# Attention with a gated feed-forward on one core: some softmax tiles turned by VectorE and DRAM in place of TensorE

## The chip, the core and the metric

The kernel runs on one of the eight cores of a Trainium2 chip. A core has TensorE (matrix products into PSUM), VectorE, ScalarE and GpSimd (element-wise work), SyncE, whose queue issues most transfers, and 16 DMA engines that carry them between DRAM and SBUF, or within either. The engines run beside each other and wait for one another by semaphores. The metric is the device time of one execution in microseconds (us).

## The reference

Eight batches, eight heads, 576 tokens, 64 columns a head. For each batch and head the scores are q k^T / 8. Scores more than tau = 0.02 below the maximum of their row are masked; a softmax follows and a product with v. The heads' results, side by side 512 wide, go through a feed-forward block with a convolution over the tokens as its gate. In short:

```
scores = scale * np.matmul(q, k.transpose(0, 1, 3, 2))
thresh = np.max(scores, axis=-1, keepdims=True) - tau
scores = np.where(scores >= thresh, scores, -1000000000.0)
scores = scores - np.max(scores, axis=-1, keepdims=True)
attn = np.exp(scores)
attn = attn / (np.sum(attn, axis=-1, keepdims=True) + 1e-09)
x = np.matmul(attn, v)                                # then heads side by side: 512 columns
h = np.maximum(x @ w_in, 0.0)                         # 512 -> 1024
conv_out[t] = sum over k of conv_w[k] * h[t + k - 1]  # 3 taps
gate = 1.0 / (1.0 + np.exp(-conv_out))
out = h * gate @ w_out                                # 1024 -> 512
```

## The kernel before

**Tiles and stages.** Heads are taken in four pairs of heads per batch, tokens in five tiles (four of 128 rows, one of 64). A batch is cut into two chunks, tiles (0, 1) and tiles (2, 3, 4). A *unit* is one tile of one pair of heads: 20 a batch, 160 in all. `unit` (from L516) makes, for each of the two heads, the scores in PSUM (L537 in batch 0 and for the 64-row tiles, L544 elsewhere, where q is held as a rounded part and a rest that are multiplied one after the other), then VectorE's maximum (L552), a limit from it (L558, or L556 on ScalarE), ScalarE's exponential (L561), VectorE's mask with the sum (L564), a few one-column instructions (L581, L585, L588) and the normalisation (L595 on ScalarE, L597 on VectorE or GpSimd). The result stands in a buffer `em` of 128 rows by 2 x 576 columns, of which there are four.

**The turn.** The product with v needs the softmax with its columns on the partitions. `transposes` (from L608) lets TensorE turn `em` in blocks of 128 x 128: two groups of four blocks per full tile, and a last group (L652) with the ninth block of each full tile and what the 64-row tile leaves over. Each group is turned into a PSUM buffer (L626), which ScalarE copies to `eT` (L621). `eT` has nine blocks by up to 320 columns for one pair of heads and one chunk; there are two such buffers.

**After the turn.** `attend` (from L664) multiplies v with `eT` (L676, L685), after the first two chunks for two pairs of heads together, and splits the result into a rounded part and a rest, `x` (L692, L695). `mm1` (L701) is the first product of the feed-forward with the convolution and the gate, whose first tap goes to an engine by the list `TAP`; `mm2` (L777) the second product, an output copy by ScalarE (L793) and the store (L794).

**Loads and copies.** All loads after the first go through SyncE's queue. `prep_k` and `prep_q` (L483, L497) load k and q for two heads, split them into a rounded part and a rest, and copy halves of them to the other 64 partitions through the queue (L477): three copies of 64 KB for q's rounded part and three for its rest. The weights, which arrive as 64-bit numbers, are taken apart by `split` (L342).

**The order.** Nothing is left to run time: a planner in the kernel (`Plan`, L87 to L242) simulates the engines while the program is built and emits each engine's instructions in the order of that simulation. Each operation is given an engine, an assumed duration, what it reads and writes, and a rank. The rank is the number of the unit it belongs to, less a lead from the table `AHEAD`, in units: 6.25 for scores, 3.5 for the turn and for the attention. An engine takes the ready operation of the lowest rank. Some operations may be taken by another engine, when the backlog of ready work on their own exceeds `BACKLOG`:

```
if e == home or load[home] + max(free[home] - t, 0.0) > BACKLOG[home]:
```

The normalisation's own engine comes from the list `NORM`, which names GpSimd alone:

```
turns = NORM[u >= NEAR]
home = turns[(u * 2 + h) % len(turns)]
```

Because the order is fixed, an operation that is late holds up all that follows on its engine's queue, SyncE's included.

Of the kernel before, what the change touches and what calls it, by code (L numbers as in the profile page):

```python
# [41 lines left out]
EARLY = 1  # L42
# [6 lines left out]

JOINT = 2  # L50

KEEP = {'rows': 2.304, 'cols': 1.613, 'turn': 3.226, 'full': 2.304}
# [30 lines left out]
class Plan:  # L83
# [32 lines left out]
    def run(self):  # L116
# [35 lines left out]
        while events:  # L152
# [25 lines left out]
            for e in ready:  # L178
# [4 lines left out]
                while ready[e]:  # L183
# [6 lines left out]
                    if e == home or load[home] + max(free[home] - t, 0.0) > BACKLOG[home]:  # L190
# [55 lines left out]
def tile_tau_attention_gated_ffn(  # L246
# [80 lines left out]
    def sp(n):  # L327
        return 2.6 * n

# [12 lines left out]
    def split(src, n, name, high, low, hr, lr, queue="sp"):  # L342
# [4 lines left out]
        value = plan.buf(wk, "q2", 2, [P, 2, 2 * P], U32, f"{name}_f")  # L347
# [8 lines left out]
        def v(dtype=F32):  # L356
            return value[:].rearrange("p a b -> p (a b)")[:, :n].bitcast(dtype)

        lo, hi, a = (stage, 0), (stage, 1), (value, 0)
        w = AHEAD["w"]  # L360

        def load():
            (nc.sync if queue == "sp" else nc.scalar).dma_start(flat().bitcast(I64), src)
# [16 lines left out]
        if queue == "sp":  # L380
            op("sp", sp(2 * n), load, w=[hi, lo], ahead=w + AHEAD["load"])
        else:
            op("act", 450, load, w=[hi, lo], ahead=90, late=sp(2 * n) + LATENCY["sp"])
# [37 lines left out]
    def load_weight(i):  # L421
        if i < W1N:
            src, dst, c, f = w_in, w1, i % NCB, i // NCB
        else:
# [4 lines left out]
            src[c * P:(c + 1) * P, f], WN, f"stage_{i}", h, l, *((x, (c, f.start)) for x in dst), "act" if i < 3 else "sp"  # L429
# [14 lines left out]
    def prep_rows(i, b, p, o, w, tag):  # L444
# [3 lines left out]
        a = AHEAD["prep"]  # L448

        if i:  # L450
            op("sp", sp(S + D), lambda: nc.sync.dma_start(k[:], kp[b, p]), w=[(k, 0), (k, 1)], ahead=a + 2)
            op("sp", sp(2 * w), lambda: nc.sync.dma_start(q[:], qd[b, p, :, :, o:o + w]), w=[(q, 0), (q, 1)], ahead=a + 2)
        else:
            for j, on in enumerate((slice(0, CH), slice(CH, S + D))):
                op(
                    "act", 450, lambda on=on: nc.scalar.dma_start(k[:, on], kp[b, p, :, on]), w=[(k, j)], ahead=210 - 10 * j,
                    late=1500 + sp(CH) * (1 + j)
                )
                op(
                    "sp", sp(w) + 400, lambda j=j: nc.sync.dma_start(q[:, j], qd[b, p, :, j, o:o + w]), w=[(q, j)], ahead=210 - 10 * j  # L460
                )
# [7 lines left out]
    def halves(dst, src, of, ahead):  # L469

        x, view, parts = src
        for part, head in of:
            j, half = part
            n = view.shape[-1]
            op(
                "sp", max(sp(n) / 2, 360),
# [6 lines left out]
    def prep_k(b, p, ks):  # L483

        a = AHEAD["prep"]
        xk = plan.buf(wk, "xk", 2, [P, S + D], F32, f"xk_{b}_{p}")
        op("sp", sp(S), lambda: nc.sync.dma_start(xk[:, :S], kt[b, p]), w=[(xk, 0), (xk, 1)], ahead=a + 2)
# [9 lines left out]
    def prep_q(i, b, p, q1, q2):  # L497

        w, o = QW, chunks[pairs[i][0]].new[0]
        xq = plan.buf(wk, "xq", 2, [P, w], F32, f"xq_{i}")  # L500
        a = AHEAD["prep"]
        op("sp", sp(w), lambda: nc.sync.dma_start(xq[:], qt[b, p, :, o:o + w]), w=[(xq, 0)], ahead=a + 2)
# [5 lines left out]
        for q in (q1, q2):  # L508
            halves(q, (q, Later(lambda q=q: q[:, 0], w), ((0, 0), (0, 1))), [((1, 1), 1), ((1, 0), 1), ((0, 1), 0)], a)
# [318 lines left out]
    def prep(i, j):  # L828
# [4 lines left out]
        if plain(b):  # L833
            if not j:
                whole[i] = (*prep_rows(i, b, p, o, w, "q1"), None)
# [119 lines left out]
```

## Time and profile before

| | |
|---|---|
| Median of 3 runs | 927.24 us (926.33 to 927.37) |
| Profiled execution | 925.54 us, span of its instructions 923.8 us |
| Granted TensorE clock, mean | 0.996 |
| Busy share of the span | TensorE 97%, VectorE 80%, ScalarE 76%, GpSimd 63% |
| Transfers | 104.02 MB in 77926 packets, mean 113 GB/s |
| HBM | 58.88 MB read, 9.44 MB written |

In the profile a line such as L626 is the line of the kernel that issued the instruction. PE is TensorE's matmuls and PEld its loads of the stationary operand, DVE is VectorE, ACT ScalarE, POOL GpSimd, SP SyncE; an engine's name with a q behind it is its queue of transfers or waits. `eT<-ps_t` reads as: writes the tile eT from the tile ps_t. Busy times within a group of instructions can overlap with those of other groups on the same engine, because instructions are pipelined.

### The profile page before, as it was taken

How to read it: one execution, taken by the hardware profiler on the slowest of the kernel's cores; microseconds unless marked ns; L12 is line 12 of the kernel's file. 1: busy time of each engine (PE TensorE's matmuls, PEld its weight loads, DVE VectorE, ACT ScalarE, POOL GpSimd, SP SyncE). 2: the span in 40 equal slices, each digit the busy share in tenths (PEclk: the TensorE clock that was granted, in tenths of full speed). 3: DMA queues.
4: the chain of work that ended last, by engine and by line, in shares of the span. 5: the costliest groups of instructions: out<-in, count | busy, mean ns of one | idle time of the engine just before them, and what ended most of it. 6: DMA issues, size and time to landing. Idle time of an engine off the chain costs nothing.

```text
span 923.8 us, 19667 instructions
## 1 busy us (share of the span) xinstructions
PE 896.7 (97%) x6308; PEld 731.8 (79%) x6308; DVE 741.1 (80%) x1853; ACT 701.2 (76%) x1590; POOL 582.1 (63%) x1028
## 2 busy tenths in 40 slices
PE   5989899999999999999999999999999999999998
PEld 2446588878889788879888787887888888887897
DVE  5988999979868798878967789886977879896643
ACT  5888898878678787869768687786958788785653
POOL 3665887767747586666746677675865757664422
PEclk9999999999999999999999999999999999999999
DMA  6643363355341652345423453416523265221000
GB/s 211 200 151 128 97 166 101 111 146 167 87 122 40 176 150 83 84 115 140 122 91 81 133 148 103 120 59 166 161 85 95 55 175 140 83 79 60 13 24 34
DMA packets 77926, 104.02 MB, mean 113 GB/s; under 512 B 18560, under 2 KB 49536, under 8 KB 77824
## 3 DMA queue, kind: packets, MB, share of 16 engines
q1 hardware_dynamic: 76960, 100.86, 38.6%
q10 hardware_dynamic: 864, 1.90, 0.6%
q8 instruction: 51, 0.84, 0.4%
q14 instruction: 51, 0.42, 0.1%
HBM read 58.88 MB, written 9.44 MB: 74 GB/s over the span
## 4 chain that ended last, share of the span: by engine, by line
PE 79%; ACT 9%; DVE 6%; issue 2%; DMA 2%; POOL 1%; SPq 0%; ACTq 0%; POOLq 0%; DVEq 0%
PE po L786 21%; PE ph L713 16%; PE ps_t L626 13%; PE pa L685 12%; PE ps_s L544 11%; PE ps_s L537 4%; ACT eT L621 2%; PE pa L676 2%; DVE em L564 2%; ACT em L561 2%; DVE few L552 1%; DVE t L748 1%; PE pw_stage L394 1%; DMA q<-in_qd_dram 1%; ACT hp L728 1%
## 5 line engine op out<-in xcount | busy, mean ns | idle before, releaser
L597 POOL TENSOR_SCALAR em<-em,few 128x576 f32<-128x576 f32 x285 | 258.3, 914 | 36.9 <-DVE few L588 27.3
L564 DVE SCALAR_TENSOR_TENSOR em<-ps_s,few,em 128x576 f32<-128x576 f32 x288 | 228.1, 812 | 51.0 <-ACT em L561 44.9
L713 PE MATMUL ph<-x,w1h 128*128 128x322 f32 (+1 forms) x1024 | 243.2, 305 | 0.7 <-ACT hp L728 0.7
L552 DVE TENSOR_REDUCE few<-ps_s 128x1 f32<-128x576 f32 x288 | 210.8, 748 | 29.4 <-PE ps_s L537 15.2
L561 ACT ACTIVATE em<-ps_s,few 128x576 f32<-128x576 f32 x288 | 206.7, 743 | 30.9 <-DVE few L552 26.0
L621 ACT ACTIVATE eT<-ps_t 128x512 f32<-128x512 f32 (+2 forms) x416 | 203.3, 512 | 16.9 <-PE ps_t L626 15.2
L626 PE MATMUL ps_t<-ident,em 128*128 128x128 f32 x1312 | 187.7, 276 | 4.6 <-DVE x L695 1.7
L626 PEld LDWEIGHTS ps_t<-ident,em 128*128 128x128 f32 x1312 | 152.3, 141 | 34.2 <-POOL em L597 11.0
L713 PEld LDWEIGHTS ph<-x,w1h 128*128 128x128 f32 x1024 | 174.9, 189 | 3.7 <-issue 1.8
L748 DVE SCALAR_TENSOR_TENSOR t<-hp,cw,t 128x255 f32<-128x255 f32 (+1 forms) x256 | 151.9, 597 | 25.9 <-ACT t L732 18.8
L544 PE MATMUL ps_s<-ks,q 128*128 128x288 f32 x896 | 155.0, 304 | 2.6 <-DVE em L564 1.6
L713 PE MATMUL ph<-x,w1l 128*128 128x322 f32 (+1 forms) x512 | 151.1, 295 | 0.0
L544 PEld LDWEIGHTS ps_s<-ks,q 128*128 128x128 f32 x896 | 129.0, 188 | 13.8 <-issue 4.6
L324 POOL TENSOR_TENSOR gl<-t,gh 128x255 fp32r<-128x255 f32 (+9 forms) x192 | 121.4, 644 | 29.4 <-ACT gh L765 29.2
L685 PE MATMUL pa<-eT,v 128*64 128x320 f32 (+1 forms) x1024 | 133.3, 412 | 0.0
L685 PEld LDWEIGHTS pa<-eT,v 128*64 128x64 f32 x1024 | 70.9, 138 | 59.9 <-issue 16.7
L786 PE MATMUL po<-w2h,gh 128*128 128x512 f32 x288 | 118.1, 410 | 0.0
L786 PE MATMUL po<-w2h,gl 128*128 128x512 f32 x288 | 113.0, 392 | 0.5 <-POOL gl L324 0.5
L786 PE MATMUL po<-w2l,gh 128*128 128x512 f32 x288 | 113.1, 393 | 0.0
L713 PEld LDWEIGHTS ph<-x,w1l 128*128 128x128 f32 x512 | 96.6, 189 | 0.1
L755 DVE SCALAR_TENSOR_TENSOR t<-t,hp 128x321 f32<-128x321 f32 (+1 forms) x128 | 70.8, 554 | 14.3 <-ACT t L757 13.6
L757 ACT ACTIVATE t<-t 128x321 f32<-128x321 f32 (+1 forms) x128 | 56.9, 445 | 24.4 <-DVE t L748 24.1
(69 smaller groups left out, 1019.6 us busy)
## 6 DMA issues: line engine op xcount, KB each, us to landing
q<-q SPq DMA_DIRECT2D x336, 64.0 KB, 2.0
v<-in_vc_dram SPq DMA_DIRECT2D x64, 288.0 KB, 3.3
k<-in_kp_dram SPq DMA_DIRECT2D x35, 320.0 KB, 3.6
out_dram<-ot SPq DMA_DIRECT2D x36, 256.0 KB, 2.0
xk<-in_kt_dram SPq DMA_DIRECT2D x28, 288.0 KB, 3.3
ks<-xk SPq DMA_DIRECT2D x56, 144.0 KB, 2.4
xq<-in_qt_dram SPq DMA_DIRECT2D x56, 128.0 KB, 2.3
stage<-in_w_out_dram SPq DMA_DIRECT2D x8, 512.0 KB, 3.5
```

The costliest lines, as they stand in the source:

```text
L324: engines[e].tensor_tensor(dst, x, y, op=ALU.subtract)
L544: nc.tensor.matmul(ps[:, c, :CH], lhsT=q[:, h, o:o + n], rhs=k[:, h, c * CH:(c + 1) * CH], start=(i == 0), stop=(i == 1))
L552: nc.vector.tensor_reduce(few[:rows, nm], ps[:rows, :, :CH], op=ALU.max, axis=mybir.AxisListType.XY, negate=True)
L561: nc.scalar.activation(view(), ps[:rows, :, :CH], AF.Exp, bias=few[:rows, nm])
L564: nc.vector.scalar_tensor_tensor(view(), ps[:rows, :, :CH], few[:rows, th], view(), op0=ALU.is_ge, op1=ALU.mult, accum_out=few[:rows, total])
L597: engines[e].tensor_scalar(sl, sl, by, to, op0=ALU.mult, op1=ALU.add)
L621: "act", act(w, True), lambda dst=dst, src=src: nc.scalar.activation(dst(), src(pt), AF.Copy),
L626: nc.tensor.transpose(out=pt[:, at:at + P], in_=em[:, int(b * P):int(b * P) + P], identity=ident[:])
L685: nc.tensor.matmul(pa[j * D:(j + 1) * D, :w], lhsT=vt[:, blk, :], rhs=eT[:, blk, :w], start=False, stop=(r == 3))
L713: nc.tensor.matmul(ph[:, :an], lhsT=w1[w][:, cb, fs], rhs=xs[cb][:, h, :an], start=(cb == 0 and i == 0), stop=(cb == NCB - 1 and i == 2))
L748: nc.vector.scalar_tensor_tensor(t[:, :kn], hp[:, k:kn + k], cw[:, 3 * f + k:3 * f + k + 1], t[:, :kn], op0=ALU.mult, op1=ALU.add)
L786: nc.tensor.matmul(po[:], lhsT=x[:, f, at:at + P], rhs=w[:, f, :], start=(f == 0 and i == 0), stop=(f == NFB - 1 and i == 2))
```

## The change

In batches 1 to 7, six of the sixteen full tiles of a batch no longer pass through TensorE. A list `SQUARES` says which of a batch's 20 units they are, and `SQFROM` that none comes before unit 24. For such a tile VectorE transposes `em` in place in squares of 32 x 32. That leaves each square turned but at its old place; the squares are put in their places by way of a DRAM buffer `sq` (four of them): four transfers write 32 partitions each into it in runs of 32 numbers (128 B), four read it back into `eT` in runs of 128 numbers (512 B). All eight go through SyncE's queue. The last group of TensorE's transposes leaves out the ninth block of such tiles.

The two parts of q become one buffer, so that three copies of 128 KB take the place of six of 64 KB. The planner's numbers change with it: leads, latencies and the assumed duration of transfers, with separate leads and backlogs for the first 24 units (`AHEAD0`, `BACKLOG0`, `HEAD`); the normalisation's own engine alternates between ScalarE (first head) and GpSimd (second head); VectorE's backlog before others may take its small instructions goes from 120 to 480 ns; the first taps are dealt out anew; the ranks of the weights' pieces and the mixing of the two products of the feed-forward change. All weights go through SyncE's queue, as does the second half of the first k. There is one output buffer in place of two, and the very last store is made in two halves.

```diff
-AHEAD = {'s': 6.25, 's4': 7.75, 't': 3.5, 'a': 3.5, 'prep': 4.25, 'w': 2.5, 'load': 7.75}
-LATENCY = {"pe": 210.0, "act": 145.0, "dve": 110.0, "pool": 75.0, "sp": 2000.0}
+AHEAD = {'s': 6.25, 's4': 8.5, 't': 3.5, 'v': 5.25, 'a': 2.0, 'prep': 5.0, 'w': 0.25, 'load': 10.0}
+AHEAD0 = {'s': 6.5, 's4': 9.25, 't': 2.0, 'v': 5.0, 'a': 3.25, 'prep': 2.0, 'w': 2.75, 'load': 7.25}
+HEAD = 24
+LATENCY = {"pe": 210.0, "act": 145.0, "dve": 110.0, "pool": 75.0, "sp": 1150.0}
-NORM = (('pool',), ('pool',))
-NEAR = 8
+NORM = (('pool', 'pool', 'pool', 'pool', 'dve', 'pool', 'act', 'act'), ('act', 'pool'))
+NEAR = 0
-TAP = ('act', 'pool', 'act', 'act')
-LOW = ('pool', 'pool')
+TAP = ('pool', 'act', 'dve', 'pool', 'act', 'act')
+LOW = ('pool',)
-MOE = (2, 2)
-BACKLOG = {'pool': 6860.0, 'dve': 120.0, 'act': 9000000000.0}
-WRATE = (1.225, 1.745)
-ALT = 11.76
+MOE = (4, 2)
+BACKLOG = {'pool': 19208.0, 'dve': 480.0, 'act': 9000000000.0}
+BACKLOG0 = {'pool': 54880.0, 'dve': 83.0, 'act': 9000000000.0}
+WRATE = (3.855, 1.12)
+ALT = 2.824
-EARLY = 1
+EARLY = 0
+SQUARES = (0, 0, 0, 0, 0, 1, 0, 0, 0, 1, 0, 0, 1, 0, 1, 1, 1, 0, 1, 0)
+SQFROM = 24
...
+    dram = ctx.enter_context(tc.tile_pool(name="dram", bufs=4, space=bass.MemoryType.DRAM))
+    def dma(n, fn, w=(), r=(), ahead=0.0):
+        op("sp", max(560, 1.3 * n), fn, w=w, r=r, ahead=ahead, late=2.9 * n - max(0, 1.3 * n - 560))
+    def lead(of):
+        return (AHEAD0 if plan.rank < HEAD else AHEAD)[of]
...
-    def prep_q(i, b, p, q1, q2):
+    def prep_q(i, b, p, q):
...
-        for q in (q1, q2):
-            halves(q, (q, Later(lambda q=q: q[:, 0], w), ((0, 0), (0, 1))), [((1, 1), 1), ((1, 0), 1), ((0, 1), 0)], a)
+        for j, half, head in ((1, 1, 1), (1, 0, 1), (0, 1, 0)):
+            dma(
+                w,
+                lambda j=j, half=half, head=head: nc.sync.dma_start(
+                    q[half * D:(half + 1) * D, :, j].bitcast(F32), q[head * D:(head + 1) * D, :, 0].bitcast(F32)
+                ),
+                w=[(q, (j, half))], r=[(q, (0, head))], ahead=a
+            )
...
+    def squares(u, n):
+        return n == P and u >= SQFROM and SQUARES[u % len(SQUARES)]
...
+        if squares(u, n):
+            a = lead("v")
+            op("dve", dve(2 * S), lambda: nc.vector.transpose(em[:], em[:]), w=[(em, 0), (em, 1)], ahead=a, port=True)
+            sq = plan.buf(dram, "sq", 4, [32, 8 * S], F32, f"sq_{u}")
+            def leave(x):
+                nc.sync.dma_start(
+                    sq[:].rearrange("j (m x i) -> x j m i", x=4, i=32)[x], em[x * 32:(x + 1) * 32, :].rearrange("j (m i) -> j m i", i=32)
+                )
+            def enter(y):
+                nc.sync.dma_start(
+                    eT[y * 32:(y + 1) * 32, :, off:off + P], sq[:].rearrange("j (k y q) -> y j k q", y=4, q=P)[y]
+                )
+            for x in range(4):
+                dma(S / 2, lambda x=x: leave(x), w=[(sq, x)], r=[(em, 0), (em, 1)], ahead=a)
+            for y in range(4):
+                dma(S / 2, lambda y=y: enter(y), w=[(eT, (off, y))], r=[(sq, x) for x in range(4)], ahead=a)
+        elif n < P:
...
-        ot = plan.buf(wk, "ot", 2, [P, DO], F32, f"ot_{m}")
+        ot = plan.buf(wk, "ot", 1, [P, DO], F32, f"ot_{m}")
...
+        x, y = slice(0, DO // 2), slice(DO // 2, DO)
+        op("act", act(DO // 2, True), lambda: nc.scalar.activation(ot[:, x], po[:, x], AF.Copy), w=[(ot, 0)], r=[(po, 0)])
+        op("dve", dve(DO // 2), lambda: nc.vector.tensor_copy(ot[:, y], po[:, y]), w=[(ot, 1)], r=[(po, 0)])
+        op("act", 450, lambda: nc.scalar.dma_start(rows[:, x], ot[:, x]), r=[(ot, 0)], late=LATENCY["sp"])
+        dma(DO // 2, lambda: nc.sync.dma_start(rows[:, y], ot[:, y]), r=[(ot, 1)])
```

More of the change, by code (lines that the diff above doesn't have):

```diff
@@ L48 @@
 }
+SQUARES = (0, 0, 0, 0, 0, 1, 0, 0, 0, 1, 0, 0, 1, 0, 1, 1, 1, 0, 1, 0)
+SQFROM = 24
 JOINT = 2
[L52 removed]
+KEEP = {'rows': 1.613, 'cols': 1.613, 'turn': 3.161, 'full': 2.304}
 class Buf:
@@ L378, in f4 @@
             nc.vector.scalar_tensor_tensor(v(U32), words()[0], 29, v(U32), op0=ALU.logical_shift_right, op1=ALU.bitwise_or)
[L380 to L383, printed above, removed]
+        dma(2 * n, load, w=[hi, lo], ahead=w + lead("load"))
         op("act", act(n), f0, w=[a], r=[hi], ahead=w)
@@ L569, in unit @@
             op(
-                "pe", 490 if q2 is None else 534, mm, w=[(ps, 0)],
-                r=[(x, j) for x in (k, q1) for j in js] if q2 is None else [(x, (h, i)) for x in (k, q1, q2) for i in range(2)], ahead=a, kind="rows" if q2 is None else "full"
+                "pe", 490 if not rounded else 534, mm, w=[(ps, 0)],
+                r=[(x, j) for x in (k, q) for j in js] if not rounded else [(x, (h, i)) for x in (k, q) for i in range(2)], ahead=a, kind="rows" if not rounded else "full"
             )
@@ L616, in group @@
             op(
-                "pe", width * 0.852, lambda: parts(pt), w=[(pt, 0)], r=reads + [(ident, 0)], ahead=AHEAD["t"], kind="turn"
+                "pe", width * 0.852, lambda: parts(pt), w=[(pt, 0)], r=reads + [(ident, 0)], ahead=lead("t"), kind="turn"
             )
```

122 lines of the change are left out of this document (67 added, 55 removed).

## The prediction

> **What bounds the kernel now.** I read the page first, then a table of engine times by stretches, then the groups of instructions, then the chain of waits, then the transfers. On the page TensorE leads both in busy time and in the chain that ended last.
>
> ```profile
> span 923.8 us, 19667 instructions
> ...
> PE 896.7 (97%) x6308; PEld 731.8 (79%) x6308; DVE 741.1 (80%) x1853; ACT 701.2 (76%) x1590; POOL 582.1 (63%) x1028
> ...
> PE 79%; ACT 9%; DVE 6%; issue 2%; DMA 2%; POOL 1%; SPq 0%; ACTq 0%; POOLq 0%; DVEq 0%
> ```
>
> The same by stretches: the start; the passage from the first batch of scores to the second; six whole batches of 20 score tiles each (195.1 to 847.5); the last of the six alone:
>
> ```profile
> core 0: us, PE busy (x) PEld busy (x) DVE busy (x) ACT busy (x) POOL busy (x), PEclk, DMA share, GB/s
> 0.00:120.00 120.00, 100.67 (x606) 60.71 (x607) 101.02 (x241) 94.41 (x196) 71.59 (x122) 0.97 0.50 157
> 97.00:195.10 98.10, 94.15 (x678) 76.05 (x680) 92.65 (x235) 82.36 (x184) 74.75 (x128) 1.00 0.43 120
> 195.10:847.50 652.40, 648.74 (x4713) 547.03 (x4711) 534.98 (x1360) 505.50 (x1159) 428.55 (x759) 1.00 0.41 113
> 738.90:847.50 108.60, 108.19 (x798) 90.70 (x796) 92.91 (x241) 85.38 (x194) 69.99 (x125) 1.00 0.40 109
> ```
>
> A batch takes 652.4 / 6 = 108.7 us. In it TensorE is busy 99.4% (108.1 us), VectorE 89.2 us (82%), ScalarE 84.2, GpSimd 71.4, the transfer engines 0.41 of the time. So a microsecond taken from TensorE is a microsecond of the batch, as long as nobody else needs more than what is left. The row from 97.00 shows another regime: VectorE 94.4% busy, TensorE down to 96.0%.
>
> **The change, part by part.** *TensorE.* A tile that VectorE turns loses its nine transposes. In the chain of waits, eight of them take:
>
> ```profile
> 510.46 0.87 PE ps_t L626 x8
> ```
>
> That is 109 ns each, so 9 x 0.109 = 0.98 us a tile, 5.9 us a batch, 41.2 us over 42 tiles. The group's busy time (187.7 us for 1312, below) would give 143 ns and 54 us, with what overlaps the neighbouring matmuls counted in. I take 109, since the chain counts only what moves the end.
>
> ```profile
> L626 PE MATMUL ps_t<-ident,em 128*128 128x128 f32 x1312 | 187.7, 276 | 4.6 <-DVE x L695 1.7 <-ACT eT L621 1.5 <-POOL em L597 1.3
> ...
> L621 ACT ACTIVATE eT<-ps_t 128x512 f32<-128x512 f32 x288 | 166.2, 602 | 14.2 <-PE ps_t L626 13.3
> ...
> L597 POOL TENSOR_SCALAR em<-em,few 128x576 f32<-128x576 f32 x285 | 258.3, 914 | 36.9 <-DVE few L588 27.3 <-DVE few L558 6.1 <-PE ps_s L544 1.1
> ...
> L595 ACT ACTIVATE em<-em,few 128x576 f32<-128x576 f32 x3 | 2.5, 880 | 0.5 <-DVE few L588 0.5
> ...
> L732 ACT ACTIVATE t<-hp,cw 128x321 f32<-128x321 f32 x48 | 27.2, 567 | 2.6 <-POOL gl L324 0.7
> ...
> L564 DVE SCALAR_TENSOR_TENSOR em<-ps_s,few,em 128x576 f32<-128x576 f32 x288 | 228.1, 812 | 51.0 <-ACT em L561 44.9 <-POOL hp L723 2.3 <-ACT few L556 1.0
> ...
> L372 DVE TENSOR_SCALAR stage_f<-stage_f 128x512 uint32<-128x512 uint32 x16 | 7.0, 438 | 2.3 <-POOL stage_f L369 2.3
> ```
>
> *VectorE.* A turn of 1152 columns in squares of 32 is not in the trace. From below, the cheapest pass over SBUF (438 ns for 512 columns) gives 0.99 us; from above, the mask (812 ns for 576) gives 1.62 us. I take 1.3, the middle, neither row being nearer in kind: 7.8 us a batch. Two taps of sixteen come to it, about 0.3 us each by half the tap's length. VectorE then needs 89.2 + 7.8 + 0.6 = 97.6 us a batch.
>
> *ScalarE.* It loses two 512-wide evictions a turned tile and some of the third, 6 x (2 x 0.602 + 0.1) = 7.8 us, and four of its twelve first taps, 4 x 0.567 = 2.3. It gains the normalisation of the first head of each of 20 tiles, since NORM now alternates and BACKLOG never lets another engine take one from ScalarE: 20 x 0.88 = 17.6. Sum 84.2 + 7.5 = 91.7 us a batch. GpSimd falls by 20 x 0.906 to about 54: slack that nothing waits for, though fewer of its instructions will hold up VectorE's.
>
> *Queue and transfers.* Per batch q's copies fall from 48 to 24 issues with the same bytes, and 48 issues are added: eight per turned tile, four writing 1152 pieces of 128 B each (4608 a tile) and four reading 288 pieces of 512 B each (1152 a tile).
>
> ```profile
> q1 hardware_dynamic: 76960, 100.86, 38.6%
> ...
> k<-in_kp_dram SPq DMA_DIRECT2D x35, 320.0 KB, 3.6
> out_dram<-ot SPq DMA_DIRECT2D x36, 256.0 KB, 2.0
> ```
>
> The queue's own durations and, for the price of a piece, two stretches of the transfers: 17.3 to 18.6 us, nearly all pieces of 256 B, and 526.5 to 530 us, mostly over 2 KB.
>
> ```profile
> L477 SPq DMA_DIRECT2D q<-q x336: 461/541/1837, 98.1 to 834.4; - x168
> ```
> ```profile
> DMA packets 324, 0.08 MB, mean 59 GB/s; under 512 B 323, under 2 KB 324, under 8 KB 324
> ...
> q1 hardware_dynamic: 324, 0.08, 26.7%
> ```
> ```profile
> DMA packets 389, 0.73 MB, mean 207 GB/s; under 512 B 77, under 2 KB 77, under 8 KB 389
> ...
> q1 hardware_dynamic: 389, 0.73, 71.5%
> ```
>
> And what SyncE's queue waited for longest:
>
> ```profile
> SPq L477 <- ACT q L503: 104.0, 26, 13.5
> ```
>
> 24 more issues of 0.54 us are 13 us of SyncE a batch. The queue now spends more than that standing before q's producers (104 us, some 15 a batch), so it has the room if the plan's order fits. A piece of 247 B took 0.267 x 16 x 1.3 us / 324 = 17 ns, one of 1.9 KB 0.715 x 16 x 3.5 / 389 = 103 ns, so by their line 512 B cost 31 ns and 128 B 11 ns; the mean piece of the whole run, 0.386 x 923.8 x 16 / 76960 = 74 ns, is the other end (a batch would then take 186 us). I take 17 for 128 B: the 247 B piece is the nearest in size, and the mean piece is ten times as long. A batch then adds 6 x (4608 x 17 + 1152 x 31) / 16 = 42.8 us of each transfer engine to 0.41 x 108.7 = 44.6: 87 of some 105 us, full but not over. A tile's chain is 1.3 (turn) + 4 x 0.54 (issue) + 2.0 (landing, as an output store) + about 3 (4608 pieces of 17 ns on 16 engines are 4.9 us, partly under the issues) + 4 x 0.54 + 3.6 (landing, as k) = 14 us. The plan puts the turn 5.25 units before its tile and the attention 2.0 before, and each turned tile has at least one more tile of its pair of heads, or of the partner pair, behind it: 4.25 units of 5.2 us, 22 us. So I cost the chain at nothing; its cover is those 8 us. Once they are gone, TensorE waits at L676 before the attention of both pairs, 28 times over batches 1 to 7, so that each microsecond of lateness costs up to 28. Behind an entering transfer that waits for its eT buffer stand the loads of k, q and v and the output stores, in queue order; these have leads of five units or more.
>
> A rule speaks against this part. The Trainium skill, "DMA: Bandwidth & Descriptors", Specifications, says that below 512 B a transfer does a read-modify-write and misses line rate. The 17 ns for 256 B here, against 31 by the line for 512, do not show it for reads; a write that short is not in this trace. By the rows the sum stands as below; by the rule (an estimate: twice the 17 ns) it would be the second rival's 984 us.
>
> *The rest.* The single copy of q waits for GpSimd's half too, where the first half's copies did not; five units of lead cover that. One output buffer in place of two makes ScalarE wait for a landing (2.0 us) between tiles of output that are over 5 us of TensorE apart; the last store in two halves gains 0.2. The retuned start can move at most the idle TensorE time of the first 120 us (first row of the stretches), 19.3 us, either way; the order there is as much replaced as kept, and I take zero with 6 us of uncertainty.
>
> **The sum.** 923.8 - 41.2 = 882.6 us if TensorE stays at 99.4%. TensorE's 108.1 - 5.9 = 102.2 us would fill a batch of 102.8, of which VectorE needs 97.6 (95%) and ScalarE 91.7 (89%). The trace has such a stretch (97.00 to 195.10) with TensorE at 96.0%; but part of its loss belongs to the weights. I take the middle, 97.7%: a batch of 104.6, 1.8 us more, 12.6 over seven batches. 882.6 + 12.6 = 895.2 us of span; the profiled execution's 925.54 stands 1.7 over its span, and the median of the runs 1.7 over that: 899 us. At 99.4% it is 886, at 96.0% 912.
>
> **The rivals.** *TensorE's whole gain arrives:* the relief from GpSimd, whose fewer instructions hold VectorE less, keeps VectorE near 90%, as in the stretch from 738.90 where 85.6% cost nothing; with a little from the start that is 880 to 886. Against it: ScalarE is at 89% too. *The written pieces fill the transfer engines (the slower side):* per batch 44.6 + 13.4 + 1.728 us for each ns a piece costs. That reaches 104.6 at 27 ns and the old 108.7 at 29 ns: from there on the kernel is slower. At 34 ns, twice 17, a batch is 116.8, +8.1 x 7 = 57, 984 us. For it: no write that short is in the trace. Against it: 17 ns for 247 B leaves room for 70% more. *VectorE becomes the bound:* its limit before GpSimd may take over its small instructions rises from 120 to 480 ns of backlog. GpSimd did these in the six batches (the row below them is the same work on VectorE, over the whole run):
>
> ```profile
> L581 POOL TENSOR_SCALAR few<-few 128x2 f32<-128x2 f32 x57 | 16.8, 294 | 27.3 <-DVE em L564 25.5
> L558 POOL TENSOR_SCALAR few<-few,ntau 128x1 f32<-128x1 f32 x45 | 15.4, 342 | 22.1 <-DVE few L552 14.5 <-DVE few L588 6.6 <-DMA v<-in_vc_dram 0.3
> L585 POOL TENSOR_SCALAR few<-few 128x2 f32<-128x2 f32 x47 | 11.4, 242 | 70.7 <-DVE em L564 69.6
> ```
> ```profile
> L558 DVE TENSOR_SCALAR few<-few,ntau 128x1 f32<-128x1 f32 x183 | 34.7, 207 | 1.0
> ```
>
> Back on VectorE at 0.2 us, these 149 are 5.0 us a batch: 102.6 us, and at the 94.4% that it has reached a batch of 108.7, about 928. The turn's upper end of 1.62 us would add 1.9. Against it: VectorE's higher load itself pushes them off.
>
> **How the numbers follow.** The likeliest case (TensorE's gain less a third) has 0.54, its own range 886 to 912. The whole gain has 0.17, VectorE as the bound 0.11, the full transfer engines 0.18. Faster by over 0.2%, which is about what a measurement of this kernel can tell from no change: 0.54 + 0.17 + 0.04 of the VectorE case = 0.75; within 0.2%, 0.06, most of it from that case; slower 0.19. The predicted time is 899. The range of 8 in 10 is 880 to 935: below lies a part of the whole gain (the 54 us price of the transposes), above most of the transfer case, together under 0.2.
>
> **What would show it.** In the changed profile L626 has 934 transposes (1312 - 378) in place of 1312; TensorE's busy time is near 855 us and its share 96 to 98% in a batch of about 104.6 us. The turns are 42 instructions near 1.3 us on VectorE, which is over 93% busy in each batch; ScalarE has some 160 normalisations near 0.88 us. The transfer share is near 0.8 and TensorE's waits name VectorE's mask or ScalarE rather than a transfer. I am wrong if a written piece takes over 27 ns and the attention waits for eT from DRAM, if VectorE's small instructions stay with it and batches stay at 108 us, or if TensorE's share stays at 99%.

## The result, and the profile after

The changed kernel is slower: 967.08 us (median of 4 runs, 964.83 to 970.6) against 927.31 us for the kernel before in the same session (926.33 to 927.84). The ratio is 1.0434, with a 95% interval of 1.0396 to 1.0471. The prediction, 899 us with a range of 880 to 935, had the wrong sign, and the range missed the time.

The lines of the page after that answer to those shown of before; the profiled execution took 964.83 us:

```profile
span 963.0 us, 19231 instructions
...
PE 890.9 (93%) x5930; PEld 705.1 (73%) x5930; DVE 782.2 (81%) x1857; ACT 752.4 (78%) x1628; POOL 473.3 (49%) x956
...
q1 hardware_dynamic: 322144, 152.04, 63.1%
...
PE 50%; DMA 12%; ACT 12%; DVE 11%; SPq 7%; issue 6%; POOL 2%; ACTq 0%; DVEq 0%; POOLq 0%
```

TensorE issues 378 instructions fewer, as it should, and yet its busy time falls by 5.8 us only and its share from 97 to 93%. In the chain that ended last TensorE has gone from 79 to 50%; transfers have 12% in place of 2, and SyncE's queue, which had nothing, has 7.

Engine times between 120 and 860 us, which is seven batches' worth of the kernel before, first after, then before:

```profile
120.00:860.00 740.00, 697.66 (x4820) 573.08 (x4819) 627.85 (x1510) 600.29 (x1309) 385.08 (x778) 0.98 0.71 172
```
```profile
120.00:860.00 740.00, 735.87 (x5336) 619.01 (x5335) 613.54 (x1560) 574.35 (x1312) 489.32 (x863) 1.00 0.41 113
```

The columns are busy us and instructions of TensorE, its weight loads, VectorE, ScalarE and GpSimd, then the granted clock, the transfer share and GB/s. VectorE stands at 627.85 / 740 = 85%, ScalarE at 81%, the transfer engines at 0.71. No engine is full, and TensorE is idle for 42 us of the 740 where it was idle for 4. So this is not a new bound but waiting. TensorE's longest waits in the changed kernel (total us, times, longest):

```profile
PE ps_s L565 <- DMA ks<-xk: 19.2, 5, 4.3
PE ps_s L558 <- DVE em L585: 9.4, 11, 2.4
PE pa L730 <- DMA eT<-sq: 6.0, 5, 3.1
```

The longest in total is in front of the scores (L565, formerly L544), for a copy of k to the other 64 partitions. This copy is not new; it has become late. The squares themselves (`eT<-sq`, ahead of the attention) make TensorE wait for 6.0 us in all.

One such wait, followed back. The chain of work from 326 us of the changed kernel, and SyncE's queue in the same stretch (start, us, what; x is the number of issues merged):

```profile
326.08 5.51 DMA sq<-em
...
331.67 0.60 SPq L674
...
333.64 0.61 SPq L674
...
334.30 3.19 DMA ks<-xk
...
337.62 2.26 PE ps_s L565 x8
```
```profile
325.47 2.07 SPq L669 DMA_DIRECT2D sq<-em  x2
327.63 1.43 SPq L491 DMA_DIRECT2D ks<-ks  x1
329.17 0.93 SPq L491 DMA_DIRECT2D ks<-xk  x1
330.14 0.63 SPq L526 DMA_DIRECT2D qq<-qq  x1
330.86 0.56 SPq L491 DMA_DIRECT2D ks<-ks  x1
331.67 2.58 SPq L674 DMA_DIRECT2D eT<-sq  x4
334.30 0.61 SPq L491 DMA_DIRECT2D ks<-xk  x1
335.00 3.13 SPq L669 DMA_DIRECT2D sq<-em  x4
```

SyncE issues without a pause for ten microseconds and more. Two writes of squares take it 2.07 us, the four reads stand until the last write has landed and take 2.58 us, and only then comes the copy of k that the scores need; TensorE had run out of work at 333.8. Waits of 3.2 to 4.3 us of this kind come five times, some 110 us apart, in five of the seven batches.

Four of the five are paid for twice. TensorE's own records around the one above:

```profile
337.62 2.26 PE L565 MATMUL ps_s<-ks,qq 128*128 128x288 f32 x8 [3.78 <-DMA ks<-xk]
...
343.86 1.23 PE L565 MATMUL ps_s<-ks,qq 128*128 128x288 f32 x8
```
```profile
328.00:333.80 5.80, 5.80 (x45) 5.21 (x43) 4.77 (x11) 5.17 (x11) 2.94 (x4) 1.00 0.81 173
333.80:337.60 3.80, 0.04 (x1) 0.01 (x1) 0.64 (x2) 1.22 (x4) 0.00 (x0) 0.80 0.87 209
337.60:344.40 6.80, 6.78 (x36) 6.79 (x37) 3.88 (x9) 3.47 (x10) 1.80 (x6) 0.61 0.91 221
```

After 3.78 us without work the same eight score products take 2.26 us, six microseconds later 1.23; the granted clock between 337.6 and 344.4 is 0.61. In the trace's record of the clock it is 0.50 from 336.1 to 342.9 us. The waits of 4.34 and 4.16 us have 6.8 us at 0.50 as well, that of 3.72 us has 3.4, and that of 3.16 us has none. The Trainium skill ("TensorE: Matmul & The Clock Gate", Part 1) says that the clock is halved after an idle window of some 3.4 us and is given back after a busy window of that length, and that these windows run freely, whatever the kernel does. The trace agrees in the halving and in the return, which came 5.3 us after work had come back. It differs in the fall, which came 2.3 us into the wait, before a whole window of idleness.

How long SyncE is held by each issue (ns, least/median/most, of the 168 of a kind):

```profile
L669 SPq DMA_DIRECT2D sq<-em x168: 550/725/2797, 153.4 to 899.0; - x168
L674 SPq DMA_DIRECT2D eT<-sq x168: 550/609/1429, 160.1 to 904.2; - x168
```

The prediction had 0.54 us for both. The writes' 168 durations add up to 142.7 us (0.85 us each), the reads' to 102.7. All issues of SyncE together take 552 us against 366 us before, 65 to 72 of every 100 us between 200 and 800 us where it had been 43 to 51.

### The profile page after: what moved, and what is told of

It reads as the page before. It is cut to its first block, busy times and chain, and to the rows that moved or that the text cites. A ratio compares the mean times of both kernels' runs of the same rounds, so it can differ in the third digit from the quotient of the medians.

```text
span 963.0 us, 19231 instructions
## 1 busy us (share of the span) xinstructions
PE 890.9 (93%) x5930; PEld 705.1 (73%) x5930; DVE 782.2 (81%) x1857; ACT 752.4 (78%) x1628; POOL 473.3 (49%) x956
## 4 chain that ended last, share of the span: by engine, by line
PE 50%; DMA 12%; ACT 12%; DVE 11%; SPq 7%; issue 6%; POOL 2%; ACTq 0%; DVEq 0%; POOLq 0%
PE ph L767 12%; PE po L840 12%; PE ps_s L565 8%; PE pa L739 8%; PE ps_t L650 6%; DVE em L585 3%; SPq L669 3%; ACT em L582 2%; SPq L674 2%; ACT em L616 2%; ACT eT L645 2%; DVE few L573 2%; DMA sq<-em 2%; PE ps_s L558 2%; DMA xk<-in_kt_dram 2%
## 5 line engine op out<-in xcount | busy, mean ns | idle before, releaser
L767 PE MATMUL ph<-x,w1h 128*128 128x322 f32 (+1 forms) x1024 | 240.0, 308 | 0.8 <-ACT ot L849 0.7
L565 PE MATMUL ps_s<-ks,qq 128*128 128x288 f32 x896 | 159.1, 310 | 31.5 <-DMA ks<-xk 19.2
L645 ACT ACTIVATE eT<-ps_t 128x512 f32<-128x512 f32 (+3 forms) x343 | 150.5, 466 | 37.0 <-PE ps_t L650 35.3
L565 PEld LDWEIGHTS ps_s<-ks,qq 128*128 128x128 f32 x896 | 131.7, 192 | 55.2 <-issue 40.1
L650 PE MATMUL ps_t<-ident,em 128*128 128x128 f32 x934 | 141.7, 280 | 12.1 <-ACT em L616 4.8
L616 ACT ACTIVATE em<-em,few 128x576 f32<-128x576 f32 x160 | 137.7, 863 | 15.1 <-DVE few L609 14.0
L618 POOL TENSOR_SCALAR em<-em,few 128x576 f32<-128x576 f32 x128 | 116.3, 908 | 48.1 <-DVE few L609 30.4
L739 PE MATMUL pa<-eT,v 128*64 128x320 f32 (+1 forms) x1024 | 137.5, 417 | 0.4 <-ACT eT L645 0.4
L650 PEld LDWEIGHTS ps_t<-ident,em 128*128 128x128 f32 x934 | 112.0, 143 | 34.6 <-ACT em L616 8.2
L579 POOL TENSOR_SCALAR few<-few,ntau 128x1 f32<-128x1 f32 x160 | 57.7, 361 | 102.0 <-DVE few L573 82.3
```

What stands on the lines that cost most here:

```text
L565: nc.tensor.matmul(ps[:, c, :CH], lhsT=q[:, i, h, o:o + n], rhs=k[:, h, c * CH:(c + 1) * CH], start=(i == 0), stop=(i == 1))
L616: nc.scalar.activation(sl, sl, AF.Identity, scale=by, bias=to)
L645: "act", act(w, True), lambda dst=dst, src=src: nc.scalar.activation(dst(), src(pt), AF.Copy),
L650: nc.tensor.transpose(out=pt[:, at:at + P], in_=em[:, int(b * P):int(b * P) + P], identity=ident[:])
L739: nc.tensor.matmul(pa[j * D:(j + 1) * D, :w], lhsT=vt[:, blk, :], rhs=eT[:, blk, :w], start=False, stop=(r == 3))
L767: nc.tensor.matmul(ph[:, :an], lhsT=w1[w][:, cb, fs], rhs=xs[cb][:, h, :an], start=(cb == 0 and i == 0), stop=(cb == NCB - 1 and i == 2))
```

## The experiments

Times are medians; the ratio is to the kernel before on the same chip, with its 95% interval. "Planner numbers" are the constants that the diff changes (`AHEAD` to `ALT`, `EARLY`, `KEEP`, and in `dma` the durations the planner believes); changing one of them gives another order of the same instructions, and with `NORM`, `TAP` and the backlogs another engine for some of them.

**Are the squares the loss at all?** First the squares alone taken out, then the squares kept with their eight transfers replaced by a copy, then that copy together with eight small transfers, then the planner told what the transfers really take.

> The changed kernel with no tile turned by VectorE (SQUARES all zero): TensorE turns all of them, and every other part of the change stays. Theory Q (SyncE's in-order queue, which now spends 0.85 us on each write to DRAM and 0.61 on each read back, makes the copies of k and q behind them late): 915 to 935 us, since the queue is relieved and TensorE has its 41 us of transposes again. Theory T (the transfer engines, 63% busy instead of 39%, land everything later): the same 915 to 935. Theory P (the new planner numbers, one output buffer and the normalisations on ScalarE are slower by themselves): 945 us or more.

```diff
-SQUARES = (0, 0, 0, 0, 0, 1, 0, 0, 0, 1, 0, 0, 1, 0, 1, 1, 1, 0, 1, 0)
+SQUARES = (0,) * 20
```

957.56 us, 1.0332 (1.0303 to 1.0361). Three quarters of the loss is there without a single square. Under it lies a second fault, in the rest of the change:

```profile
120.00:860.00 740.00, 719.17 (x5143) 597.07 (x5142) 592.68 (x1528) 640.12 (x1405) 367.17 (x707) 1.00 0.42 111
```

TensorE is idle for 21 of 740 us at a transfer share of 0.42, and all issues of SyncE take 281 us in this run, so nothing here comes from the queue's new load.

> The changed kernel with the eight transfers of a turned tile replaced by one GpSimd copy from em to eT. The squares are left in the wrong places: this leaves out the moving of squares between partitions. VectorE still turns, TensorE still leaves out 378 transposes. Theories Q and T: 885 to 905 us, TensorE's gain is there as soon as the transfers are gone. Theory P: 940 us or more. If VectorE and ScalarE at 95 and 89% are what holds TensorE: 905 to 920.

```diff
-            for x in range(4):
-                dma(S / 2, lambda x=x: leave(x), ...)
-            for y in range(4):
-                dma(S / 2, lambda y=y: enter(y), ...)
+            op("pool", 1900, lambda: nc.gpsimd.tensor_copy(eT[:, :, off:off + P], em[:].rearrange("p (k q) -> p k q", q=P)), ...)
```

938.26 us, 1.0123 (1.0095 to 1.0152): 19 us faster than without squares, on a GpSimd that has time to spare. The copy leaves the squares where they are, so it shows what TensorE's time is worth, not a way of moving them. VectorE's turn does give time of TensorE back (878.1 us busy in place of 910.7 without squares) once SyncE's queue no longer carries the squares.

> As the kernel with the GpSimd copy, but with the eight transfers kept beside it, each cut to a ninth of its bytes (four of 36 squares written, one of nine blocks read back): the same number of issues on SyncE's queue, the same waits, a ninth of the pieces. The copy puts in what the cut transfers leave out, squares in wrong places. Theory Q: 940 to 967 us, since issues and waits stay. Theory T: 890 to 910 us, as with the GpSimd copy.

```diff
+                    sq[:].rearrange(...)[x][:, 0:4], em[...].rearrange("j (m i) -> j m i", i=32)[:, 0:4]
...
+                    eT[y * 32:(y + 1) * 32, 0:1, off:off + P], sq[:].rearrange(...)[y][:, 0:1]
...
+            op("pool", 1900, ...)        # and the copy of the run before
```

935.46 us, 1.0085 (1.0055 to 1.0115). That lies outside both expectations. Eight more transfers a tile, with the waits between them but a ninth of the pieces, cost nothing. The issues of the writes took 0.43 us at the median, and SyncE 430 us in all, 143 more than with the copy alone (287). So in this order neither the number of transfers nor 143 us more of the queue is a loss. The landings are not cleared by this run, for they were shorter too: 1.6 and 1.9 us at the median in place of 3.3 and 3.1.

> The changed kernel, with the planner told the durations that its own trace shows: 0.85 us of the queue for a write to DRAM and 0.62 for every other issue (assumed: 0.56), landing 3.1 to 3.3 us after the issue (assumed: 2.5 for the squares). Same work, other order. Theory Q in the form that the order is wrong because the planner believes the queue to be faster than it is: 905 to 940 us. Theory Q in the form that the queue has no room: 955 to 970. Theory T: 955 to 970, since no order makes the transfer engines less busy.

```diff
+        op("sp", 620 if cost is None else cost, fn, w=w, r=r, ahead=ahead, late=1300)
...
+                dma(S / 2, lambda x=x: leave(x), ..., cost=850)
```

951.92 us, 1.0267 (1.0235 to 1.03). An order made with the measured durations recovers 15 us, not the whole, and lies between the two expectations.

**What costs 30 us without squares?** All planner numbers put back, without and with squares:

> The changed kernel with the planner's numbers of before (leads, latencies, transfer durations, NORM, TAP, MOE, backlogs, WRATE, KEEP) and no tile turned by VectorE. What stays of the change is its structure: q copied as one, one output buffer, the weights on SyncE's queue, the split last store. Theory P1 (the 30 us of the run without squares come from the numbers): 920 to 935 us. Theory P2 (they come from the structure): 945 to 960.

> The same with the six squared tiles a batch, turned 5.25 units ahead: VectorE, transfers and TensorE do what they do in the changed kernel, the normalisations stay on GpSimd. Theory P1: the squares by themselves are worth what TensorE saves less what the queue costs, 900 to 930 us, below the run without them. Theory Q: the queue holds up k and q whatever the numbers are: 940 to 970, above the run without them.

```diff
-AHEAD = {'s': 6.25, 's4': 8.5, 't': 3.5, 'v': 5.25, 'a': 2.0, 'prep': 5.0, 'w': 0.25, 'load': 10.0}
+AHEAD = {'v': 5.25, 's': 6.25, 's4': 7.75, 't': 3.5, 'a': 3.5, 'prep': 4.25, 'w': 2.5, 'load': 7.75}
...
-        op("sp", max(560, 1.3 * n), fn, w=w, r=r, ahead=ahead, late=2.9 * n - max(0, 1.3 * n - 560))
+        op("sp", max(2.6 * n, 360), fn, w=w, r=r, ahead=ahead)
```

Without squares 935.4 us, 1.0102 (1.0071 to 1.0133); with squares 955.51 us, 1.0317 (1.0283 to 1.0352). Where the 8 us of the first come from is seen in where the scores of batch 1 begin. The row of L565 (L544 before) of before, of this kernel, and of the one that has the new numbers without squares:

```profile
L544 PE MATMUL ps_s<-ks,q x896: 288/295/402, 116.7 to 857.1; 128*128 128x288 f32 x180
```
```profile
L565 PE MATMUL ps_s<-ks,qq x896: 288/296/442, 124.2 to 867.0; 128*128 128x288 f32 x180
```
```profile
L565 PE MATMUL ps_s<-ks,qq x896: 288/296/577, 117.1 to 889.5; 128*128 128x288 f32 x180
```

With the old numbers the new structure (single copy of q, the weights on SyncE's queue, one output buffer) starts 7.5 us later, and has then 867.0 - 124.2 = 742.8 us for the seven batches against 740.4 before. With the new numbers the start is as early as before, and the seven batches take 772.4. So the new numbers repair the start and cost 30 us in the batches (772.4 - 742.8). Between the pages of these two runs, 8.9 us of it all is longer busy time of TensorE for the same 6308 products (910.7 against 901.8 us) and 13.2 us idle time; no group of TensorE's waits in the slower run is longer than 8.3 us in all, so no single wait stands for the loss.

With squares and old numbers TensorE's time goes elsewhere:

```profile
PE ps_t L650 <- POOL em L618: 20.7, 25, 2.2
PE ph L767 <- ACT hp L782: 7.8, 6, 2.0
```

Here GpSimd still has all normalisations and comes late with them. SyncE's issues took 537 us in this kernel too; how its 20 us over the run without squares divide between the two was not separated.

> The changed kernel with one number put back: NORM names GpSimd for all normalisations again. Theory N (the 160 normalisations on ScalarE, 0.86 us each, are what costs the 30 us): 925 to 942 us. If another number or the structure does: 955 to 970.

> The changed kernel without squares and with NORM back on GpSimd. Theory N: 920 to 935 us, as before the change (against 957.6 without squares and with ScalarE's normalisations). If another number or the structure does: 945 to 960.

```diff
-NORM = (('pool', 'pool', 'pool', 'pool', 'dve', 'pool', 'act', 'act'), ('act', 'pool'))
+NORM = (('pool',), ('pool',))
```

973.77 us, 1.0517 (1.0482 to 1.0553), and without squares 960.69 us, 1.0364 (1.0328 to 1.04). Moving the normalisations back to GpSimd helps in neither, though ScalarE falls from 84 to 73% without squares. My theory that ScalarE's new work is the loss falls.

> The changed kernel without squares, and with the planner's belief about transfers as it was before: 2000 ns of latency behind a transfer and 2.6 ns a column on the queue, in place of 1150 ns and max(560, 1.3 ns a column). Theory B (the order is wrong because the planner believes that k's and q's copies land earlier than they do): 932 to 942 us, near the 935 of the old numbers, against 957.6. If the leads or the other numbers (MOE, TAP, NORM, backlogs) cost the 22 us: 950 to 960.

> The changed kernel without squares, and with the leads as they were before (AHEAD, for the first 24 units too); the new beliefs about transfers stay. Theory L (attention 2.0 in place of 3.5 units ahead and the others): 932 to 942 us. Theory B or the other numbers: 950 to 960.

> Both at once: transfer times and leads of before, the rest of the numbers (NORM, TAP, LOW, MOE, backlogs, WRATE, ALT, KEEP, EARLY) as changed, no squares. If B and L are the cause between them: 930 to 942 us. If the rest of the numbers is: 950 to 960.

```diff
 # the first and the third (all three with SQUARES = (0,) * 20)
-LATENCY = {"pe": 210.0, "act": 145.0, "dve": 110.0, "pool": 75.0, "sp": 1150.0}
+LATENCY = {"pe": 210.0, "act": 145.0, "dve": 110.0, "pool": 75.0, "sp": 2000.0}
...
+        op("sp", max(2.6 * n, 360), fn, w=w, r=r, ahead=ahead)
 # the second and the third
+AHEAD = {'v': 5.25, 's': 6.25, 's4': 7.75, 't': 3.5, 'a': 3.5, 'prep': 4.25, 'w': 2.5, 'load': 7.75}
+AHEAD0 = AHEAD
```

946.86 us, 1.0215 (1.0198 to 1.0232), with the old transfer times; 948.16 us, 1.023 (1.0211 to 1.025), with the old leads; 942.01 us, 1.0161 (1.014 to 1.0182), with both. Against 957.56 they give back 10.7, 9.4 and together 15.6 us: about half of what the numbers cost in the batches. The first two lie between their expectations. The rest lies in the other numbers and was not taken apart, and why the new leads and transfer times make a slower order was not followed further.

**What do the squares cost on the queue?** The next two have the changed kernel's planned order exactly, since the planner is told the same. In the first each write puts 32 whole rows of 4608 B in place of 1152 pieces of 128 B, so that the squares come back in wrong places; bytes, issues and waits are those of the change. The second adds to it, behind each write, a transfer of 4 KB that nobody reads.

> The changed kernel with its squares, where each of the four writes of a turned tile puts whole rows of 4608 B into the DRAM buffer in place of 36 pieces of 128 B; bytes, issues and waits stay, and the squares come back in wrong places. Theory T in the form that the number of pieces costs (193536 pieces of 128 B go): 940 to 952 us. Theory T in the form that it is bytes and landings whatever the pieces are: 960 to 970.

```diff
-                    sq[:].rearrange("j (m x i) -> x j m i", x=4, i=32)[x], em[x * 32:(x + 1) * 32, :].rearrange("j (m i) -> j m i", i=32)
+                    sq[:].rearrange("j (x n) -> x j n", x=4)[x], em[x * 32:(x + 1) * 32, :]
```

> The kernel with whole rows written (926.7 us), and behind each of the four writes of a turned tile one more transfer of 4 KB that nobody reads: 168 more issues of about 0.42 us on SyncE's queue, the time that the pieces cost there, in the same planned order; squares in wrong places. Theory QT (the pieces cost through the queue's issue time): 950 to 970 us, the loss is back. Theory T (through the transfer engines and the landing of the data): 925 to 935.

```diff
+                nc.sync.dma_start(sq[:].rearrange("j (x n) -> x j n", x=4)[x], em[x * 32:(x + 1) * 32, :])
+                nc.sync.dma_start(dm[x], em[x * 32:(x + 1) * 32, 0:32])
```

With long rows 926.72 us, 1.0005 (0.9986 to 1.0024), 40 us less than the change and less than either expectation; with the added issues 964.38 us, 1.0408 (1.0369 to 1.0446). The page, the issues and the longest wait for a transfer, first with long rows, then with the added issues:

```profile
span 924.7 us, 19241 instructions
...
PE 878.2 (95%) x5930; PEld 696.5 (75%) x5930; DVE 782.1 (85%) x1857; ACT 752.5 (81%) x1628; POOL 471.7 (51%) x956
```
```profile
L669 SPq DMA_DIRECT2D sq<-em x168: 302/421/1722, 153.4 to 861.2; - x168
```
```profile
PE ps_s L565 <- DMA ks<-xk: 7.0, 4, 2.8
```
```profile
span 965.9 us, 19535 instructions
...
PE 892.4 (92%) x5930; PEld 705.3 (73%) x5930; DVE 784.3 (81%) x1857; ACT 753.3 (78%) x1628; POOL 470.9 (49%) x956
```
```profile
L671 SPq DMA_DIRECT2D dm<-em x168: 303/420/1924, 154.3 to 903.3; - x168
```
```profile
PE ps_s L565 <- DMA ks<-xk: 13.9, 4, 4.6
PE ps_s L565 <- DMA dm<-em: 8.7, 2, 4.4
```

A write of whole rows holds SyncE for 0.42 us in place of 0.725 (74.3 us in all in place of 142.7). Its pieces on the transfer engines are fewer as well; the landings of other transfers did not get shorter (the copy of k took 3.3 us with long rows, 3.0 in the changed kernel), while the squares' own writes landed sooner (2.8 us at the median in place of 3.3). The second run tells issue time from pieces and landings: it keeps the long rows, its writes land in 2.2 us, and its 168 added issues, which add up to 75.3 us, raise SyncE's total from 467 to 546 us (the change: 552), while the transfer share between 120 and 860 us is 0.64. The loss is back to within 3 us, in front of the same line. (Nobody reads dm: in the two waits put down to it, the copy of k that was issued just before it landed 0.1 us before TensorE went on.) So in this order the time that the issues hold SyncE is shown to be enough for 38 of the 40 us, and neither the short pieces on the transfer engines nor the landings are needed for it. Of the 38.3 us between the spans of the change and of the long rows, 25.6 are TensorE's idle time ((963.0 - 890.9) - (924.7 - 878.2)) and 12.7 a longer busy time for the same instructions. The granted clocks give about as much: their mean was 0.979 and 0.993 in these two profiles, and (1 - 0.979) x 963.0 - (1 - 0.993) x 924.7 = 13.7 us, an estimate.

An added microsecond of issues has no fixed price: the run with small pieces carried 143 of them for nothing. One reading fits the runs, though none tests it alone. The new numbers let the planner believe 0.56 us for each of a tile's eight issues. On average they took 0.43 us with small pieces and 0.53 with long rows; they took 0.73 in the change, and 0.76 where each write has a second issue behind it. By this reading what lasts longer than planned makes all that stands behind it late. With the old numbers, which believe 0.75 us, waits for a copy of k are not among TensorE's longest. But the order told the true durations won back 15 us only.

**Can the queue be relieved?** Three kernels send the loads of k, q and v through another queue; one turns fewer tiles.

> The changed kernel with its squares and pieces, but the loads of k, q and v from DRAM (29 a batch, about 15 us of the queue) issued by GpSimd, which is 49% busy. Theory QT: 930 to 950 us. Theory T: 960 or more, the bytes and pieces are the same. If GpSimd's own issues cost it more than 1.5 us each, it is no test, and its busy time shows that.

> The changed kernel with the same loads on ScalarE's queue, where ScalarE is 78 to 85% busy with half the normalisations. Theory QT: 930 to 950 us, less than the other gains since ScalarE comes near 95%. If ScalarE becomes the bound: 960 or more.

> Squares, the planner's numbers of before (955.5 us so far), and the loads of k, q and v from DRAM issued by ScalarE's queue: about 0.45 us each there, 29 a batch, on an engine that is 73% busy in this version. SyncE's queue goes from 67 to about 52 us in 100. Theory QT: 920 to 940 us, the best version with squares. If it is landings and not the queue: 950 to 960.

```diff
+        op("pool", 1000, fn, w=w, r=r, ahead=ahead, late=2500)              # by GpSimd
...
+        op("act", 450, fn, w=w, r=r, ahead=ahead, late=LATENCY["sp"] + 2.9 * n)   # by ScalarE
...
-        dma(S, lambda: nc.sync.dma_start(xk[:, :S], kt[b, p]), ...)
+        load2(S, lambda: nc.scalar.dma_start(xk[:, :S], kt[b, p]), ...)
```

The diff shows one of the five loads that move. By GpSimd the time is 1070.17 us, 1.1567 (1.153 to 1.1604); by ScalarE 1033.57 us, 1.1148 (1.1103 to 1.1193); by ScalarE with the old numbers 1044.17 us, 1.1258 (1.1223 to 1.1294). SyncE's issues did fall to 438 us by ScalarE, and all three missed by far what the theory of the queue expected. GpSimd's issues took it 0.56 to 0.76 us each on average, under the 1.5 that the expectation allowed, but in its order the loads of k (L505) waited for 83 us in all. With the loads on ScalarE:

```profile
ACT ot L853 <- DMA out_dram<-ot: 34.7, 10, 6.1
...
ACT hp L786 <- DMA ks<-xk: 19.9, 3, 7.6
```

An activation (hp, of the feed-forward) that reads no transfer waits up to 7.6 us for a copy of k. The wait is that of a load ahead of it in ScalarE's order, for a buffer that the copy still reads: one such activation started at 611.42 us, 7.55 us after ScalarE's last work, and the load of the next k had been issued at 611.04, just ahead of it. The computation behind a load stands with it. That spoils these runs as a test of the queue: they neither support nor refute it. Whether this wait accounts for the whole loss stays open.

> The changed kernel with three squared tiles a batch in place of six. The queue has 35 us less to issue over the run, TensorE 20.6 more to do. Against 957.6 with none and 967.1 with six: a straight line between them gives 962. If lateness on the queue grows faster than its load (theory QT): 945 to 955, below both.

```diff
+SQUARES = (0, 0, 0, 0, 0, 1, 0, 0, 0, 0, 0, 0, 0, 0, 1, 0, 0, 0, 1, 0)
```

975.21 us, 1.0499 (1.0446 to 1.0552): three tiles a batch are worse than six and than none, outside both expectations, with SyncE's issues at 414 us only. So the queue's total is no law across orders. This kernel has another plan, and its longest wait is another one (the transposes for the split of x, 15.6 us). The queue's price holds for the order in which it was measured.

> The kernel before with one output buffer in place of two, nothing else. If the 8 us that stay with the old numbers and no squares come from the output buffer: 932 to 938 us. If from the single copy of q or the start: 925 to 929.

```diff
-        ot = plan.buf(wk, "ot", 2, [P, DO], F32, f"ot_{m}")
+        ot = plan.buf(wk, "ot", 1, [P, DO], F32, f"ot_{m}")
```

In the kernel before: 926.22 us, 0.9998 (0.998 to 1.0015). The single output buffer costs nothing.

No version with squares was faster than the kernel before.

## Why the prediction was wrong, point by point

The terms of the sum that it derived from rows of durations held. The rows after:

```profile
L650 PE MATMUL ps_t<-ident,em 128*128 128x128 f32 x934 | 141.7, 280 | 12.1 <-ACT em L616 4.8 <-ACT eT L645 4.3 <-DVE x L749 2.4
L616 ACT ACTIVATE em<-em,few 128x576 f32<-128x576 f32 x160 | 137.7, 863 | 15.1 <-DVE few L609 14.0 <-DVE few L579 0.8 <-POOL few L606 0.2
...
L664 DVE STREAM_TRANSPOSE em<-em 128x1152 f32<-128x1152 f32 x42 | 57.6, 1371 | 7.1 <-POOL em L618 5.9 <-POOL hp L777 0.6 <-ACT em L616 0.4
```

- *TensorE's 378 transposes*: 934 are left, as foreseen. What they are worth can be seen where the issues are short: 957.56 - 926.72 = 31 us of the 41.2, though these two kernels also differ in order. TensorE's busy time, 890.9 us where 855 was foreseen, goes the same way: 896.7 before, 14.0 more with the rest of the change alone (910.7), 32.5 less with squares and long rows (878.2), 12.7 more with the short pieces.
- *The turn* took 1.371 us (1.3, bounds 0.99 to 1.62), the 160 normalisations 0.863 us (0.88). Both right. Neither VectorE nor ScalarE became the bound: 85 and 81% in the batches, where 93 and more were foreseen for VectorE, because the batches became longer.
- *The written pieces*: in one microsecond in which nearly nothing else moved,

```profile
DMA packets 1260, 0.16 MB, mean 159 GB/s; under 512 B 1260, under 2 KB 1260, under 8 KB 1260
...
q1 hardware_dynamic: 1260, 0.16, 95.1%
```

  a piece of about 127 B took 0.951 x 16 x 1.0 us / 1260 = 12 ns, close to the 11 ns of the line and under the 17 taken. The rule of the Trainium skill that was weighed ("DMA: Bandwidth & Descriptors", Specifications) would have had it at 34 by the prediction's estimate, which reads it as a doubling; no such doubling shows here. That short pieces miss line rate does show: 127 B in 12 ns are 10.6 B a ns, 1.9 KB in 103 ns were 18. The transfer share came to 0.71, under the 0.8 foreseen. The rival with full transfer engines had the right sign, but not by its mechanism.
- *The chain of 14 us within 22 us of lead* held nearly: the attention waited for squares for 6.0 us in all, where each microsecond of lateness was priced at 28.
- *The queue is the step that failed.* "24 more issues of 0.54 us are 13 us of SyncE a batch ... so it has the room" took the duration of a copy with few pieces for a write of 1152 pieces. Measured: 0.85 and 0.61 us; the new issues are (142.7 + 102.7) / 7 = 35 us a batch, of which 11 were saved at q's copies ((182.2 - 107.2) / 7). The 104 us that the queue had stood before q's producers were not room either: they lie where the plan put them, while the k copies came late behind squares. "These have leads of five units or more" was the second half of the error: the lead is a rank, not a time, and in SyncE's fixed order the copies of k stand behind reads that stand behind landings.
- *"The retuned start ... I take zero with 6 us of uncertainty"* is the other step that failed. It gave the new numbers a term for the start and none for the batches. Without squares they cost 22 us on top of the structure's 8, and 30 us in the seven batches alone. I had looked for their effect in the start, where they are worth 7 us the other way, and not in the batches, whose order they replace as well.

In short, from 927 us: +8 for the structure with old numbers, +22 for the new numbers (957.6), -31 with squares whose issues are short (926.7), +40 with short pieces (967), of which the time that issues hold SyncE is shown to be enough for 38.

## What to carry to other kernels

Price a transfer three times: on its engines, in its landing, and in the time its issue holds the queue. The last was longer here for more pieces of the same bytes (0.42 us for a write of 32, 0.725 for one of 1152) and was paid by what stood behind it in order, copies that were not part of the change. A queue's idle time is no room unless it lies ahead of the transfer that is needed next; and issue time has no fixed price (143 us more cost nothing in one order, 78 us more cost 38 in another), so measure it in the order that will run. When a change comes with retuned planner numbers, treat them as a change of the whole order, with a range of tens of microseconds either way, and measure them apart.

## What the hardware showed that I had not expected

An issue of 1152 pieces held SyncE for 0.725 us at the median and up to 2.8, one of the same bytes in 32 rows for 0.421. Whether the difference is the making of the pieces' descriptors or a full ring behind them was not separated. The second has something for it: with short pieces the loads of v, which did not change, took 0.54 us of SyncE at the median, with long rows 0.40; but with squares and old numbers, short pieces too, they took 0.43.

The cost of a wait of TensorE does not end with it: after 3.78 us the clock granted over the next 6.8 us was 0.61, and that part of the loss shows as busy time, not as idle time. After a wait of 3.16 us, 450 us later, the clock stayed at 1.00.
